# Inverse Fourier transform along the tokens with k and -k in two halves of the partitions, exchanged by DMA and combined before a real-matrix product

## The chip, the core and the metric

The kernel runs on one core of a Trainium2 chip. The metric is the device time of one execution in microseconds (us); the median of three runs of the kernel before is 484.28 us (483.43 to 484.54).

## What is computed

The input x has 2048 tokens of 448 features. It is normalized per token, and three things are added: x itself, a gated network of the normalized input, and a spectral filter of it.

```python
xn = layernorm(x)
X  = rfft2(xn, axes=(tokens, features))      # 2048 x 225 complex
A  = irfft2(X * (w_r + 1j * w_i))            # 2048 x 448 real
gate, up = xn @ W_gate, xn @ W_up            # 448 -> 1792
B  = (gate * (gate > 0) * up) @ W_down       # 1792 -> 448
out = x + A + B
```

The change is in the inverse transform along the tokens, a part of A.

## The kernel before

**The two works.** The gated network is the foreground: 56 units of two wide products each (`gu_unit`, 14 blocks of 128 hidden features times four chunks of 512 tokens), written as fp16 high and low parts so that three fp16 products stand for one fp32 product, and products back to 448 columns (`dn_mm`, 48 of them). After each unit ACT and DVE turn its PSUM tile into `h` (`gu_post`); that tile has two buffers, so unit i+2 waits for the post of unit i. The spectral filter is the background: a list `bg` of steps, each with a cost. `run_bg` hands them out after each foreground unit, in the list's order, so many cost units for each unit; the pace is the sum of all costs divided by the foreground's length. A scheduler then lays each engine's instructions out, and each engine runs its own list strictly in order. All loads and stores are issued by SP, in one list too.

**The spectral filter.** The 2048 tokens are split as 16 n1 + n2. Forward: a transform along the features (`f_dft`), one along n1 by matrices of 128 x 128 (`f_sdft`, six stationary matrices for each n2), and four stages of butterflies over n2 on DVE (`bfly`). Then 16 products with the weights (`wmul`, the weights come by `load_wf`), the four butterfly stages backwards (`inv1`, `stage2`, `stage3`, `stage4`), which give one tile U for each n2, [128 partitions of k1, 4 groups x 2 (real, imaginary) x 57], and then, for each n2, a chain of seven steps, the list `il`:

- `i_hi` (ACT, line 460) and `i_lo` (DVE, lines 466 and 467): U as fp16 high and low part into `vt`, which has two buffers. Line 467 writes a negated copy of the imaginary part beside them, so that `vt` holds (-imaginary, real, imaginary) for each group.
- `i_sdft` (PE, line 479): the complex transform along k1. `vt` is stationary, the constant `im` (cosine and sine, high and low: four 128 x 128 matrices, loaded by `load_im`, line 453, three buffers) moves. For each of four groups three products with the cosine and three with the sine: 24 matmuls for each n2.
- `i_pq`, `i_pqlo` (ACT and DVE, lines 485 to 498), `i_ddft` (PE, line 507, 12 matmuls), `i_acc` (DVE, line 512): the inverse along the features, added onto the output tile `xy`.

In step t of that part each item of `il` runs for another n2, the last item first, and every second step begins with a `stage4` that makes two tiles U.

```python
seq = ((0, cw, 0), (0, cw, 2), (1, cw, 0), (0, sw, 1), (0, sw, 3), (1, sw, 1))
for i, (h, w, c) in enumerate(seq):
    P.matmul(o, v[:, h, w], m[:, c, :], start=(i == 0), stop=(i == 5), skip_group_check=True)
```

The names of the lines in the profile: L590 and L597 `gu`, L638 `dn`, L479 `i_sdft`, L507 `i_ddft`, L332 to L336 `f_sdft`, L623 and L626 the DVE part of `gu_post`, L644 `dn_post`, L343 to L367 the butterflies, L438 to L441 `wmul`.

Of the kernel before, what the change touches and what calls it, by code (L numbers as in the profile page):

```python
# [9 lines left out]
F16 = mybir.dt.float16  # L10
F32 = mybir.dt.float32
# [8 lines left out]
KC = 57  # L20
GW = 2 * KC
XW = 4 * GW
VW = 3 * KC
VT = 700
GROUPS = [5, 5, 4]
BGEND, LAG, AHEAD, RAMP = 10, 1, 3, 5
NWARM = 24
# [34 lines left out]
    return off, GW * 15  # L62


def _constants():
# [46 lines left out]
    ident = np.eye(128, dtype=np.float16)  # L112
    return dict(ident=ident, c_fd=c_fd, c_fm=c_fm, c_im=c_im, c_id=np.ascontiguousarray(c_id))


@with_exitstack
def tile_gfnet_reglu(ctx: ExitStack, tc: tile.TileContext, x, xr, wgu, wd, wf, ident, c_fd, c_fm, c_im, c_id, out):
    nc = tc.nc
    V, A, P, G = nc.vector, nc.scalar, nc.tensor, nc.gpsimd

# [206 lines left out]
    def f_sdft(n2):
        ps = fx()
        y = ps[:, 0:XW].rearrange("p (g c k) -> p g c k", g=4, c=2)
        m, xh = fm_t[n2], Xh[n2]  # L330
        for i, (a, b) in enumerate(((0, 0), (0, 1), (3, 0))):
            P.matmul(y, m[:, a, :], xh[:, b], start=(i == 0), stop=False, skip_group_check=True)  # L332
        for a, b in ((1, 0), (1, 1), (4, 0)):
            P.matmul(y[:, :, 0], m[:, a, :], xh[:, b, :, 1], start=False, stop=True, skip_group_check=True)  # L334
        for a, b in ((2, 0), (2, 1), (5, 0)):
            P.matmul(y[:, :, 1], m[:, a, :], xh[:, b, :, 0], start=False, stop=True, skip_group_check=True)  # L336
        yps[n2] = y

    def bfly(a, b, p, sgn):

# [108 lines left out]
    sps, pg, pgh, vt = {}, {}, {}, {}  # L449

    def load_im(n2):
        im_t[n2] = it([128, 4, 128], F16, "im", 3)
        nc.sync.dma_start(im_t[n2], c_im[n2])

    def i_hi(n2):
        v = vt[n2] = state["vt"][state.setdefault("vn", 0) % 2]
        state["vn"] += 1
        u = cur["U", n2].rearrange("p g c k -> p g (c k)")
        g = v[:, :, 0:4 * VW].rearrange("p h (g w) -> p h g w", g=4)
        A.activation(g[:, 0, :, KC:], u, AF.Copy, scale=fsc[:, 0:1])  # L460

    def i_lo(n2):
        ut = cur.pop(("U", n2))
        u = ut.rearrange("p g c k -> p g (c k)")
        g = vt[n2][:, :, 0:4 * VW].rearrange("p h (g w) -> p h g w", g=4)
        V.scalar_tensor_tensor(g[:, 1, :, KC:], u, fsc[:, 0:1], g[:, 0, :, KC:], op0=OP.mult, op1=OP.subtract)  # L466
        V.tensor_scalar(g[:, :, :, 0:KC], g[:, :, :, 2 * KC:], -1.0, None, op0=OP.mult)
        free.append(ut)

    def i_sdft(n2):  # L470
        ps = fx()
        v, m = vt[n2], im_t[n2]
        for g in range(4):
            o = ps[:, 128 * g:128 * (g + 1)]
            cw = slice(VW * g + KC, VW * g + KC + 128)
            sw = slice(VW * g, VW * g + 128)
            seq = ((0, cw, 0), (0, cw, 2), (1, cw, 0), (0, sw, 1), (0, sw, 3), (1, sw, 1))
            for i, (h, w, c) in enumerate(seq):
                P.matmul(o, v[:, h, w], m[:, c, :], start=(i == 0), stop=(i == 5), skip_group_check=True)  # L479
# [225 lines left out]
    fft_chunk(3)  # L705
    add(0.3, wmax_scale)
    add(0.0, open_inv)
    add(0.0, lambda: nc.sync.dma_start(idc_t, c_id))
    ks = [0, 4, 2, 6, 1, 5, 3, 7]
    korder = [k for k0 in ks for k in (k0, k0 + 8)]  # L710
# [1 line left out]
        add(0.0, load_wf, k)  # L712
    add(0.0, wneg, korder[0])
    nload = 3
    for k0 in ks:
        add((1.1, 1.7, 1.7, 1.7, 1.2, 1.7, 1.7, 1.7)[k0], stage4, k0, 1, "s3", "X")
        for k in (k0, k0 + 8):
            i = korder.index(k)
            if i + 1 < 16:
                add(0.0, wneg, korder[i + 1])  # L720
            add(1.7, wmul, k)
            if nload < 16:
                add(0.0, load_wf, korder[nload])
                nload += 1
        add(1.1, inv1, k0)
        if k0 >= 4:
            for par in range(2):
                add(1.1 + 0.1 * par, stage2, k0 - 4, par, -1, "i1", "i2")
            if k0 - 4 >= 2:
                for k in range(4):  # L730
                    add((1.1, 1.7, 1.2, 1.7)[k], stage3, k0 - 6, k, -1, "i2", "i3")
# [267 lines left out]
```

## Time and profile before

| what | value |
|---|---|
| median of three runs | 484.28 us |
| the profiled execution's own time | 483.15 us |
| its span, first to last instruction | 481.2 us |
| mean granted TensorE clock | 0.991 |
| inverse transforms on PE (L479) | 346.95 to 453 us of the span |
| foreground left behind the last background matmul | 460.4 to 477.5 us |

A profile shows one execution. For each engine it gives the time in which it was busy; the views used below are the page's summary, the stretches (busy time of each engine in a piece of the span), the timeline (instructions in order of time: start, duration, engine, line, operation, tiles, count), the waits (who waited for whom), the chain of waits that ended last, and the DMA issues with their time to landing. A matmul's duration in it includes the way through the array, so what one costs PE in a row of many is the distance from start to start, not that duration. PEld is TensorE's weight load, SPq is SP's list of DMA issues.

### The profile page before, as it was taken

The page shows a single profiled execution, that of the slowest core. Times are in us where ns is not written, and L with a number is a line of the kernel's source. Part 1 is how long each engine was busy: PE and PEld are TensorE (multiplying, and loading weights), DVE is VectorE, ACT ScalarE, POOL GpSimd, SP SyncE. Part 2 cuts the span into 40 slices and gives each one's busy share as a digit, 9 for nine tenths or more (in the row PEclk, how much of TensorE's full clock was granted, in tenths as well). Part 3 has the DMA queues.
Part 4 walks back from the last instruction along what each step waited for, and adds up shares of the span by engine and source line. Part 5 has one row for each costly group of instructions (what it writes and reads, how often), then busy time and mean ns, then how long its engine had stood idle before and what let it go on. Part 6 is the DMA issues. An engine that isn't in the chain of part 4 may idle for free.

```text
span 481.2 us, 7678 instructions
## 1 busy us (share of the span) xinstructions
PE 467.2 (97%) x2896; PEld 245.6 (51%) x2896; DVE 384.3 (80%) x934; ACT 170.3 (35%) x341; POOL 28.9 (6%) x62
## 2 busy tenths in 40 slices
PE   8769999999999999999999999999999999999996
PEld 3424455455545555554444444444556565665653
DVE  6779369568964999989999999999998677676632
ACT  5846225132442742332122043442253243333310
POOL 2104004000300100000000000001000000000000
PEclk9898999999999999999999999999999999999999
DMA  7999300601501355150212011200011100020012
GB/s 262 385 380 230 121 1 17 138 0 34 121 1 44 125 173 166 53 180 21 59 41 58 1 39 40 64 2 0 1 33 32 42 23 11 23 72 30 26 71 97
DMA packets 35293, 38.70 MB, mean 80 GB/s; under 512 B 15302, under 2 KB 31430, under 8 KB 35256
## 3 DMA queue, kind: packets, MB, share of 16 engines
q1 hardware_dynamic: 35256, 38.21, 26.0%
q8 instruction: 23, 0.38, 0.3%
q14 instruction: 14, 0.11, 0.1%
HBM read 31.38 MB, written 3.67 MB: 73 GB/s over the span
## 4 chain that ended last, share of the span: by engine, by line
PE 80%; issue 8%; DMA 3%; DVE 2%; ACT 1%; SPq 1%; POOL 0%; POOLq 0%; ACTq 0%
PE gu L590 42%; PE dn L638 24%; PE fx L479 4%; PE fx L507 3%; PE gu L597 3%; PE fx L290 2%; DMA T<-tt 2%; PE fx L332 1%; DMA wst<-in_wgu 1%; PE fx L334 1%; PE fx L336 1%; ACT wt L549 1%; SPq L264 1%; DVE wdm L555 1%; DVE wt L550 0%
## 5 line engine op out<-in xcount | busy, mean ns | idle before, releaser
L590 PE MATMUL gu<-T,wt 128*128 128x512 f16 (+1 forms) x1140 | 257.0, 378 | 4.6 <-DVE T L278 2.8
L590 PEld LDWEIGHTS <-wt 128*128 128x128 f16 x1140 | 109.9, 98 | 134.8 <-issue 14.9
L638 PE MATMUL dn<-wdt,h 128*128 128x448 f16 x672 | 134.8, 352 | 0.0
L638 PEld LDWEIGHTS <-h 128*128 128x128 f16 x672 | 65.4, 98 | 60.7 <-issue 1.3
L622 ACT ACTIVATE g<-gu 128x512 f32<-128x512 f32 x56 | 33.3, 595 | 119.2 <-PE gu L597 70.3
L623 DVE SCALAR_TENSOR_TENSOR g<-gu,g 128x512 f32<-128x512 f32 x56 | 38.4, 685 | 23.0 <-ACT g L622 22.9
L625 ACT ACTIVATE h<-g 128x512 f16<-128x512 f32 x56 | 35.0, 626 | 37.6 <-DVE g L623 35.3
L644 DVE SCALAR_TENSOR_TENSOR xy<-dn,dsc,xy 128x448 f32<-128x448 f32 x48 | 32.4, 679 | 18.1 <-PE dn L638 18.1
L626 DVE TENSOR_TENSOR h<-g,h 128x512 f16<-128x512 f32 x56 | 38.4, 686 | 9.8 <-ACT h L625 9.6
L466 DVE SCALAR_TENSOR_TENSOR vt<-y,fsc,vt 128x456 f16<-128x456 f32 x16 | 11.0, 690 | 17.8 <-ACT vt L460 17.8
L479 PEld LDWEIGHTS <-vt 128*128 128x128 f16 x384 | 22.7, 98 | 3.5
L479 PE MATMUL fx<-im,vt 128*128 128x128 f16 x384 | 23.9, 219 | 0.0
L549 ACT ACTIVATE wt<-wst,wsc 128x512 f16<-128x512 f32 x28 | 18.9, 712 | 13.3 <-DVE wsc L541 11.8
L550 DVE SCALAR_TENSOR_TENSOR wt<-wst,wsc,wt 128x512 f16<-128x512 f32 x28 | 20.4, 745 | 3.4 <-ACT wt L549 3.4
L597 PE MATMUL gu<-T,wt 64*128 64x512 f16 x112 | 17.0, 381 | 4.2 <-DVE wt L550 4.0
L527 ACT ACTIVATE junk<-wst 128x512 bf16<-128x512 f32 x28 | 17.4, 622 | 6.1 <-DMA wst<-in_wgu 5.8
L495 ACT ACTIVATE pgh<-pg 114x512 f16<-114x512 f32 x16 | 10.1, 628 | 26.4 <-DVE pg L493 26.4
L460 ACT ACTIVATE vt<-y,fsc 128x456 f16<-128x456 f32 x16 | 10.7, 674 | 22.3 <-PE fx L479 22.3
L530 POOL PARTITION_ALL_REDUCE wm<-wm x15 | 7.3, 485 | 160.0 <-ACT junk L527 160.0
L507 PE MATMUL fx<-idc_t,pgh 114*128 114x112 f16 (+1 forms) x192 | 16.6, 236 | 0.0
L322 ACT ACTIVATE Xh<-X 128x456 f16<-128x456 f32 x16 | 9.3, 579 | 18.5 <-DVE X L320 9.5
L344 DVE TENSOR_TENSOR y<-y,y 128x456 f32<-128x456 f32 x22 | 13.9, 630 | 0.5
(102 smaller groups left out, 458.0 us busy)
## 6 DMA issues: line engine op xcount, KB each, us to landing
wst<-in_wgu SPq DMA_DIRECT2D x28, 256.0 KB, 4.2
wmx<-in_wf SPq DMA_DIRECT2D x16, 228.0 KB, 2.7
wf<-in_wf SPq DMA_DIRECT2D x16, 228.0 KB, 2.5
y<-in_xr SPq DMA_DIRECT2D x16, 224.0 KB, 5.0
xy<-in_x SPq DMA_DIRECT2D x16, 224.0 KB, 5.1
out<-xy SPq DMA_DIRECT2D x16, 224.0 KB, 1.9
wdst<-in_wd SPq DMA_DIRECT2D x14, 224.0 KB, 4.1
fm<-in_c_fm SPq DMA_DIRECT2D x16, 192.0 KB, 2.6
```

The lines of the kernel that those rows point to most:

```text
L479: P.matmul(o, v[:, h, w], m[:, c, :], start=(i == 0), stop=(i == 5), skip_group_check=True)
L507: P.matmul(ps[:, o0:o1], h[:, a, i, :], idc_t[:, b, c0:c0 + o1 - o0], start=(j == 0 and i < 3), stop=True, skip_group_check=True)
L549: A.activation(w[:, 0:4, :], st, AF.Copy, scale=sc)
L550: V.scalar_tensor_tensor(w[:, 4:8, :], st, sc, w[:, 0:4, :], op0=OP.mult, op1=OP.subtract)
L590: last["P"] = P.matmul(hps[f, q][:, g, cs], wt[f, g][:, a, :], Tq[q][:, b, cs], start=(start and i == 0), stop=(stop and i == len(seq) - 1 ...
L597: m = P.matmul(hps[f, q][:, g, 0:512], wt[f, g][rows, 7, :], Tq[q][rows, b, :], start=start, stop=not start).ins
L622: last["A"] = A.activation(g1, hps[f, q][:, 0, :], AF.Relu, scale=2.0 ** -22).ins
L623: last["V"] = V.scalar_tensor_tensor(g1, hps[f, q][:, 1, :], 2.0 ** -22, g1, op0=OP.mult, op1=OP.mult).ins
L625: A.activation(h[:, 0, :], g1, AF.Copy)
L626: V.tensor_tensor(h[:, 1, :], g1, h[:, 0, :], op=OP.subtract)
L638: last["P"] = P.matmul(ps[:, 0:D], ht[f, q][:, a, js], wdt[f][:, b, :], start=(i == 0), stop=(i == n - 1)).ins
L644: last["V"] = V.scalar_tensor_tensor(xy[:, n2, :], dps[n2][:, 0:D], dsc[:, g:g + 1], xy[:, n2, :], op0=OP.mult, op1=OP.add).ins
```

## The change

The frequencies are laid out anew over the partitions: partition p holds k1 = p for p up to 64, and k1 = -(p - 64) for p from 65 to 127. So k and -k are 64 partitions apart. The forward matrices of the upper half have sine and cosine in each other's place, so that the forward half runs the same instructions on other constants. In the inverse half:

- `i_swap` (new, SP): for each n2 three DMAs: row 64 of U is replaced by a row of a tile `row` (line 510), partitions 65 to 127 of U go to partitions 1 to 63 of a tile t (line 513), and 1 to 63 to 65 to 127 (line 514). There are three tiles t, in the place of the weight buffers `wf`.
- `i_pair` (new, DVE, lines 518 and 519): two operations of 128 x 228 that subtract and add t.
- `i_lo` loses the negated copy; `vt` holds each group once.
- `i_sdft` has three matmuls for each group, 12 for each n2, with one real matrix (high and low); `load_im` loads half as much.
- Row 64 (k1 = 64, its own partner) takes another way: after each `wmul` a DMA copies it to one of 16 partitions of `row` (`row_in`, line 482); once, `row_hi`, `row_lo` and `row_dft` put it through a 16-point transform (nine matmuls of the forms of `f_sdft`) and `row_ev` writes it back to `row`.
- The background steps stand in another order around this: `inv1` and what follows for one k come a step later, behind the next `wmul`; `load_im` comes two steps later. The costs of the steps are changed, most of them raised (butterflies of 1.7 count 2.0, `wmul` 2.0).

```diff
+    def row_in(k2):
+        if "row" not in state:
+            state["row"] = it([16, 4, 2, KC], F32, "row")
+        nc.sync.dma_start(state["row"][k2:k2 + 1], cur["V", k2][64:65])
...
+    def row_dft():
+        ps = fx()
+        y = state["rowps"] = ps[0:16, 0:XW].rearrange("p (g c k) -> p g c k", g=4, c=2)
+        cdft(y, row_t, state["rowh"])
...
+    def i_swap(n2):
+        u = cur["U", n2]
+        nc.sync.dma_start(u[64:65], state["row"][n2:n2 + 1])
+        t = sw[n2] = state["sw"][state.setdefault("swn", 0) % 3]
+        state["swn"] += 1
+        nc.sync.dma_start(t[1:64], u[65:128])
+        nc.sync.dma_start(t[65:128], u[1:64])
+
+    def i_pair(n2):
+        u, t = cur["U", n2], sw[n2]
+        V.tensor_tensor(u[:, :, 0], u[:, :, 0], t[:, :, 1], op=OP.subtract)
+        V.tensor_tensor(u[:, :, 1], u[:, :, 1], t[:, :, 0], op=OP.add)
...
-        V.tensor_scalar(g[:, :, :, 0:KC], g[:, :, :, 2 * KC:], -1.0, None, op0=OP.mult)
...
-            seq = ((0, cw, 0), (0, cw, 2), (1, cw, 0), (0, sw, 1), (0, sw, 3), (1, sw, 1))
-            for i, (h, w, c) in enumerate(seq):
-                P.matmul(o, v[:, h, w], m[:, c, :], start=(i == 0), stop=(i == 5), skip_group_check=True)
+            w = slice(GW * g, GW * g + 128)
+            for i, (h, c) in enumerate(((0, 0), (0, 1), (1, 0))):
+                P.matmul(o, v[:, h, w], m[:, c, :], start=(i == 0), stop=(i == 2), skip_group_check=True)
...
-    il = ((0.0, i_hi), (0.8, i_lo), (0.0, i_sdft), (1.4, i_pq), (0.6, i_pqlo), (0.0, i_ddft), (0.7, i_acc))
+    il = ((0.0, i_swap), (0.8, i_pair), (0.0, i_hi), (0.7, i_lo), (0.0, i_sdft), (1.4, i_pq), (0.7, i_pqlo),
+          (0.0, i_ddft), (0.7, i_acc))
```

Two places of the order show what moves. The first is DVE's list at the first inverse transforms of the kernel before, from the last `stage4` butterfly (L343, L344, which write two tiles U, here `y_81` and `y_71`) to the end of `i_lo` for the first of them.

```order
L343 TENSOR_TENSOR y_81<-y_74,y_71 128x456
L344 TENSOR_TENSOR y_71<-y_74,y_71 128x456
L623 SCALAR_TENSOR_TENSOR g_3731<-gu,g_3731 128x512
L466 SCALAR_TENSOR_TENSOR vt_2538<-y_81,fsc,vt_2538 128x4x114
L466 SCALAR_TENSOR_TENSOR vt_2539<-y_71,fsc,vt_2539 128x4x114
L467 TENSOR_SCALAR vt_2538<-vt_2538 128x2x4x57
```

In the changed kernel the same place reads as follows; `y_68` is the first tile U, L685 and L688 are `gu_post`, L706 is `dn_post`, L380 and L381 belong to the next butterfly, `wf` is the tile t.

```order
L363 TENSOR_TENSOR y_68<-y_74,y_71 128x456
L706 SCALAR_TENSOR_TENSOR xy<-dn,dsc,xy 128x448
L364 TENSOR_TENSOR y_71<-y_74,y_71 128x456
L688 TENSOR_TENSOR h<-g_3554,h 128x512
L706 SCALAR_TENSOR_TENSOR xy<-dn,dsc,xy 128x448
L380 SCALAR_TENSOR_TENSOR y_74<-y_81 128x4x57
L381 SCALAR_TENSOR_TENSOR y_74<-y_81 128x4x57
L518 TENSOR_TENSOR y_68<-y_68,wf 128x4x57
L519 TENSOR_TENSOR y_68<-y_68,wf 128x4x57
L386 SCALAR_TENSOR_TENSOR y_81<-y_74,y_75 128x456
L387 SCALAR_TENSOR_TENSOR y_75<-y_74,y_75 128x456
L531 SCALAR_TENSOR_TENSOR vt_2442<-y_68,fsc,vt_2442 128x456
```

Between the write of U and the fp16 low part there stand now six other rows, then the pair (L518, L519), then two rows of the next butterfly. The second place is SP's list where the inverse transforms begin. Before, it holds loads of weights and of `im` only:

```order
L175 DMA wst<-in_wgu 128x512 x2
L453 DMA im<-in_c_im 128x512 x4
L648 DMA out<-xy 128x448
L453 DMA im<-in_c_im 128x512
L648 DMA out<-xy 128x448
```

In the changed kernel (L510, L513, L514 the three DMAs of a swap, L473 `load_im`):

```order
L195 DMA wst<-in_wgu 128x512 x2
L482 DMA row<-y_71 1x12x38
L510 DMA y_68<-row 1x12x38
L513 DMA wf<-y_68 63x456
L514 DMA wf<-y_68 63x456
L510 DMA y_71<-row 1x12x38
L513 DMA wf<-y_71 63x456
L514 DMA wf<-y_71 63x456
```

Where two loads and no transfer inside the core stood, three transfers for each n2 stand now: five swaps follow one another so, and behind them `load_im` and the stores of `out` stand among the swaps.

More of the change, by code (lines that the diff above doesn't have):

```diff
@@ L22 @@
 XW = 4 * GW
-VW = 3 * KC
-VT = 700
+VT = XW + 14
 GROUPS = [5, 5, 4]
@@ L62, in _fd_parts, with _freqs @@
     return off, GW * 15
+def _freqs():
+    p = np.arange(128)
+    k1 = np.where(p < 64, p, np.where(p == 64, 64, 64 - p))
+    return (k1[None, :] + 128 * np.arange(16)[:, None]) % S
 def _constants():
@@ L325, in f_lo, with cdft @@
         V.tensor_tensor(Xh[n2][:, 1], X[n2], Xh[n2][:, 0], op=OP.subtract)
[L327 to L330, printed above, removed]
+    def cdft(y, m, xh):
         for i, (a, b) in enumerate(((0, 0), (0, 1), (3, 0))):
@@ L336, in f_sdft @@
             P.matmul(y[:, :, 1], m[:, a, :], xh[:, b, :, 0], start=False, stop=True, skip_group_check=True)
-        yps[n2] = y
+    def f_sdft(n2):
+        y = yps[n2] = fx()[:, 0:XW].rearrange("p (g c k) -> p g c k", g=4, c=2)
+        cdft(y, fm_t[n2], Xh[n2])
     def bfly(a, b, p, sgn):
@@ L451, in load_im, with row_hi, row_lo, row_ev @@
     def load_im(n2):
-        im_t[n2] = it([128, 4, 128], F16, "im", 3)
+        im_t[n2] = it([128, 2, 128], F16, "im", 3)
         nc.sync.dma_start(im_t[n2], c_im[n2])
+    def row_in(k2):
+        if "row" not in state:
+            state["row"] = it([16, 4, 2, KC], F32, "row")
+        nc.sync.dma_start(state["row"][k2:k2 + 1], cur["V", k2][64:65])
+    def row_hi():
+        h = state["rowh"] = it([16, 2, 4, 2, KC], F16, "rowh")
+        A.activation(h[:, 0], state["row"], AF.Copy, scale=fsc[0:16, 0:1])
+    def row_lo():
+        h = state["rowh"]
+        V.scalar_tensor_tensor(h[:, 1], state["row"], fsc[0:16, 0:1], h[:, 0], op0=OP.mult, op1=OP.subtract)
+    def row_dft():
+        ps = fx()
+        y = state["rowps"] = ps[0:16, 0:XW].rearrange("p (g c k) -> p g c k", g=4, c=2)
+        cdft(y, row_t, state["rowh"])
+    def row_ev():
+        V.tensor_scalar(state["row"], state["rowps"], small[0:16, 19:20], 2.0 ** -10, op0=OP.mult, op1=OP.mult)
+    def open_swap():
+        state["sw"] = [it([128, 4, 2, KC], F32, "wf", 3) for _ in range(3)]
+        for t in state["sw"]:
+            for p in (0, 64):
+                G.memset(t[p:p + 1], 0.0)
+    sw = {}
+    def i_swap(n2):
[9 more added lines that the diff above has]
+        V.tensor_tensor(u[:, :, 1], u[:, :, 1], t[:, :, 0], op=OP.add)
     def i_hi(n2):
@@ L457, in i_hi @@
         state["vn"] += 1
-        u = cur["U", n2].rearrange("p g c k -> p g (c k)")
-        g = v[:, :, 0:4 * VW].rearrange("p h (g w) -> p h g w", g=4)
-        A.activation(g[:, 0, :, KC:], u, AF.Copy, scale=fsc[:, 0:1])
+        u = cur["U", n2].rearrange("p g c k -> p (g c k)")
+        A.activation(v[:, 0, 0:XW], u, AF.Copy, scale=fsc[:, 0:1])
     def i_lo(n2):
         ut = cur.pop(("U", n2))
[L464 to L467, printed above, removed]
+        u = ut.rearrange("p g c k -> p (g c k)")
+        v = vt[n2]
+        V.scalar_tensor_tensor(v[:, 1, 0:XW], u, fsc[:, 0:1], v[:, 0, 0:XW], op0=OP.mult, op1=OP.subtract)
         free.append(ut)
@@ L714, in tile_gfnet_reglu, with back @@
     nload = 3
-    for k0 in ks:
-        add((1.1, 1.7, 1.7, 1.7, 1.2, 1.7, 1.7, 1.7)[k0], stage4, k0, 1, "s3", "X")
+    def back(k0):
+        add(1.2, inv1, k0)
+        if k0 >= 4:
+            for par in range(2):
+                add(1.25 + 0.3 * par, stage2, k0 - 4, par, -1, "i1", "i2")
+            if k0 - 4 >= 2:
+                for k in range(4):
+                    add((1.25, 2.0, 1.55, 2.0)[k], stage3, k0 - 6, k, -1, "i2", "i3")
+    for i0, k0 in enumerate(ks):
+        add((1.25, 2.0, 2.0, 2.0, 1.55, 2.0, 2.0, 2.0)[k0], stage4, k0, 1, "s3", "X")
         for k in (k0, k0 + 8):
@@ L720, in tile_gfnet_reglu @@
                 add(0.0, wneg, korder[i + 1])
-            add(1.7, wmul, k)
+            add(2.0, wmul, k)
+            add(0.0, row_in, k)
             if nload < 16:
@@ L724, in tile_gfnet_reglu @@
                 nload += 1
[L725 to L731, printed above, removed]
-    il = ((0.0, i_hi), (0.8, i_lo), (0.0, i_sdft), (1.4, i_pq), (0.6, i_pqlo), (0.0, i_ddft), (0.7, i_acc))
+        if i0:
+            back(ks[i0 - 1])
+    add(0.0, open_swap)
+    add(0.0, row_hi)
+    add(0.6, row_lo)
+    back(ks[-1])
+    add(0.0, row_dft)
+    add(0.6, row_ev)
+    il = ((0.0, i_swap), (0.8, i_pair), (0.0, i_hi), (0.7, i_lo), (0.0, i_sdft), (1.4, i_pq), (0.7, i_pqlo),
+          (0.0, i_ddft), (0.7, i_acc))
     io = [n for n0 in range(8) for n in (n0, n0 + 8)]
@@ L735, in tile_gfnet_reglu @@
         if t < 16 and t % 2 == 0:
-            add(1.7, stage4, t // 2, -1, "i3", "U")
-        if t < 16:
-            add(0.0, load_im, io[t])
+            add(2.0, stage4, t // 2, -1, "i3", "U")
+        if 2 <= t < 18:
+            add(0.0, load_im, io[t - 2])
         for st in reversed(range(len(il))):
```

35 lines of the change are left out of this document (23 added, 12 removed).

## The prediction

> **What bounds the kernel now.** I read the page's busy times first, then its chain of waits, then the stretches.
>
> ```profile
> PE 467.2 (97%) x2896; PEld 245.6 (51%) x2896; DVE 384.3 (80%) x934; ACT 170.3 (35%) x341; POOL 28.9 (6%) x62
> ...
> PE 80%; issue 8%; DMA 3%; DVE 2%; ACT 1%; SPq 1%; POOL 0%; POOLq 0%; ACTq 0%
> ```
>
> PE is busy in 97% of the span and makes 80% of the chain that ended last; DVE makes 2%. The stretches say where the missing 3% are (length, then busy time of PE, PEld, DVE, ACT, POOL, each with its count; granted clock, DMA share, GB/s).
>
> ```profile
> 0.00:40.00 40.00, 30.30 (x160) 15.57 (x161) 30.50 (x101) 24.80 (x53) 7.64 (x29) 0.91 0.96 334
> ...
> 240.00:280.00 40.00, 40.00 (x197) 18.07 (x196) 38.56 (x79) 9.07 (x19) 0.00 (x0) 1.00 0.11 30
> 280.00:320.00 40.00, 40.00 (x199) 18.22 (x198) 39.35 (x92) 17.96 (x41) 2.23 (x4) 1.00 0.15 43
> 320.00:345.00 25.00, 25.00 (x125) 11.36 (x124) 24.69 (x53) 6.51 (x11) 1.83 (x1) 1.00 0.00 1
> 345.00:370.00 25.00, 25.00 (x209) 15.22 (x207) 22.59 (x57) 11.67 (x22) 0.00 (x0) 1.00 0.08 23
> 370.00:400.00 30.00, 30.00 (x249) 18.23 (x248) 20.55 (x49) 9.55 (x18) 0.00 (x0) 1.00 0.10 34
> ```
>
> PE idles 9.7 us in the first 40 us, which the change does not touch; in the rows from 240 to 400 us it idles not at all, at full clock. DVE nearly fills 240 to 345 us (102.6 of 105 us) and then has slack: 2.4 us in 345 to 370, 9.5 us in the next 30. So what PE no longer has to do in the inverse part shortens the kernel, as long as DVE, which gets more to do just behind its fullest stretch, does not make PE wait there.
>
> **What goes.** The timeline of PE around one inverse transform (start, duration, what, count):
>
> ```profile
> 357.35 1.50 PE L479 MATMUL fx<-im,vt 128*128 128x128 f16 x24
> 358.69 1.03 PE L507 MATMUL fx<-idc_t,pgh 114*128 114x112 f16 x12
> ...
> 360.19 4.27 PE L590 MATMUL gu<-T,wt 128*128 128x512 f16 x19
> 364.30 1.50 PE L479 MATMUL fx<-im,vt 128*128 128x128 f16 x24
> ```
>
> From start to start 24 matmuls take 1.34 us, 55.8 ns each (the 1.50 us hold the way through the array behind the last one). The change takes 12 of 24 in each of 16 transforms: 192 x 55.8 ns = **10.7 us** of PE. PE is the bound there, so all of it counts. The Trainium skill ("TensorE: Matmul & The Clock Gate", section "Back-to-back issue gap") gives about 81 ns as the sustained distance of such 128-column matmuls with their weight loads; by it 15.6 us would go and the result, all else as below, would be near 471 us on the scale of the median. This trace has 55.8 ns, weight loads included, and the trace decides.
>
> On DVE the negated copy goes: 16 operations, each 0.19 us from start to start (first two rows below), 3.0 us. Half the loads of `im` go too; they were early anyway and are worth nothing.
>
> **What comes on PE.** `row_dft` has nine matmuls of the three forms of one `f_sdft`, three of each; it has fewer partitions, but what streams is as wide.
>
> ```profile
> 112.69 0.74 PE L332 MATMUL fx<-Xh,fm 128*128 128x456 f16 x3
> 113.27 0.47 PE L334 MATMUL fx<-Xh,fm 128*128 128x228 f16 x3
> 113.58 0.46 PE L336 MATMUL fx<-Xh,fm 128*128 128x228 f16 x3
> 113.88 0.92 PE L638 MATMUL dn<-wdt,h 128*128 128x448 f16 x4
> ```
>
> From the first row's start to the last row's that is **1.19 us**, once. PE's balance is 10.7 - 1.2 = 9.5 us less.
>
> **What comes on DVE, and what hides it.**
>
> ```profile
> 342.82 0.28 DVE L467 TENSOR_SCALAR vt<-vt 128x456 f16<-128x456 f16 x1
> 343.01 0.39 DVE L360 SCALAR_TENSOR_TENSOR y<-y 128x228 f32<-128x228 f32 x1
> 343.31 0.39 DVE L361 SCALAR_TENSOR_TENSOR y<-y 128x228 f32<-128x228 f32 x1
> ```
>
> `i_pair` has two fp32 operations of 128 x 228; such an operation takes 0.39 us, 0.30 from start to start. 32 of them are 9.6 us, and `row_lo` and `row_ev` are as long as a 456-wide operation, 0.55 each (L344 to L623 below): 10.7 us come, 3.0 go, 7.7 us more, 0.5 us in each step of the inverse part. A step takes some 7 us (357.35 to 364.30 above), so 370 to 400 us hold about four, and DVE idles 9.45 us there, 2.4 us a step; each step also gets 0.67 us shorter. About 1.2 us a step of cover are left, so in the steady part I count the pairs at nothing. Were that cover gone, their 9.6 us would be PE's.
>
> **The swap's wait.** No plain copy from SBUF to SBUF has a row here. The loads of `im` land 2.0 us after their issue, those of `wf` 2.5, the transposing transfers within SBUF 3.3, and the slowest `fm` 5.2 (minimum, median, maximum in the fourth row; the fifth is that of `im`); the last row gives SP's spacing, (2.16 - 0.33)/3 = 0.61 us from one issue to the next.
>
> ```profile
> im<-in_c_im SPq DMA_DIRECT2D x16, 128.0 KB, 2.0
> wf<-in_wf SPq DMA_DIRECT2D x16, 228.0 KB, 2.5
> ...
> T<-tt SPq DMA_TRANSPOSE x12, 3.3
> ...
> DMA to landing us min/median/max: 2.2/2.6/5.2
> DMA to landing us min/median/max: 1.9/2.0/3.2
> ...
> 21.03 2.16 SPq L169 DMA_DIRECT2D y<-in_xr  x4
> ```
>
> A swap's third DMA is issued 1.2 us after the first and lands 2.0 to 2.5 us later: 3.2 to 3.7 us after U is written. I take 3.5, since a half moves 115 KB and transposes nothing, nearest to `im`; bounds 3.1 (1.9, `im`'s shortest and no row's less) and, with 5.2, 6.4; as slow as a transpose it would be 4.5. L518 stands in DVE's list and waits for it, with the posts L685 and L688 queued behind it and PE's next units waiting for those. In the order quoted above, the first L518 has seven rows between U's write and itself, the write counted: two `dn_post` and one `gu_post` operation of 0.60, two butterflies of 0.55, two of 0.30, in all 3.5 us. So the first swap is just covered at 3.5, short by 1.0 us at 4.5 and by 2.9 us at 6.4. On SP the swap queues `load_im` and `out` behind it: `im` has three buffers and was ready long before, and eleven stores stand behind the last swap in any case. `row_in` stands before `load_wf` on SP and waits for `wmul`, whose next weights are three tiles ahead: nothing.
>
> **The first transforms** are the tight place. Before:
>
> ```profile
> 339.79 0.63 DVE L343 TENSOR_TENSOR y<-y,y 128x456 f32<-128x456 f32 x1
> 340.46 0.64 DVE L344 TENSOR_TENSOR y<-y,y 128x456 f32<-128x456 f32 x1
> 340.63 1.23 ACT L460 ACTIVATE vt<-y,fsc 128x456 f16<-128x456 f32 x2
> 341.01 0.68 DVE L623 SCALAR_TENSOR_TENSOR g<-gu,g 128x512 f32<-128x512 f32 x1
> 341.61 1.29 DVE L466 SCALAR_TENSOR_TENSOR vt<-y,fsc,vt 128x456 f16<-128x456 f32 x2
> ...
> 346.95 2.84 PE L479 MATMUL fx<-im,vt 128*128 128x128 f16 x48
> ```
>
> U is written from 339.79, the negated copy ends at 342.82 + 0.28 = 343.10, PE comes at 346.95: 3.85 us of cushion. In the changed kernel the chain from U's write is 3.5 us to the pair, 0.7 for the pair, 0.6 for ACT's high part and 0.7 for the low part (both as before), 5.5 us instead of 3.3: 2.2 us of the cushion go. `row_lo` and `row_ev` take 1.1 more. Left are 0.5 us. How much later DVE gets there because the raised costs hand the background out faster, into a stretch that is 98% full, no row shows. I take **1.0 us** of waiting, near the 0.5 us of cushion; bounds 0 (the cushion holds; waiting cannot gain) and 6 us: a landing of 5.2 us is 2.9 us short at the first swap, and again at the fourth, which needs the first one's tile t.
>
> **The sum**, against the profiled execution's own 483.15 us: -10.7 + 1.2 + 1.0 = -8.5 us, 474.6 us. The median stands 1.13 us above that execution, and so I forecast **475.7 us** for the median.
>
> **The rivals.**
>
> *DVE makes the first stretch longer.* For it: 24.69 of 25 us busy in 320 to 345 us, three swap tiles, U tiles that come two at a time. Against it: the cushion of 3.85 us. Decided by a landing near a transpose's 3.3 us with a DVE that arrives 2 us later: 4 to 5 us lost instead of 1, 478 to 479 on the own scale, about 479.5 for the median. Chance 0.19.
>
> *The exchange becomes the bound: slower.* Each of the 16 pairs waits for its swap. Between U's write and its pair stand 5 to 27 rows of DVE in the changed order, 4.7 us on average by the durations above; DVE's spare 1.2 us a step lie on top. To eat 9.5 us, each step has to lose 0.6 us, so the swap must take 6.5 us, a landing of 5.3 us every time; at a landing of 6.5 us it would be 16 x (1.2 + 6.5 - 5.9) = 29 us against 9.5 gained, near 504 us. For it: only `fm`'s slowest row. Against it: the DMA share there is 0.08 to 0.10, against 0.96 where loads took longest. Chance 0.06.
>
> *PE is not the bound.* Its 97% would be a share of overlapping durations, and the 9.5 us would turn into idle time: 483 to 484 us, no change. The trace speaks against it: 19 `gu` matmuls take 4.11 us from 360.19 to 364.30, 216 ns each, without a gap, and 216 + 55.8 and the like fill every stretch. Chance 0.04. In the Trainium skill, "Perfetto Trace Analysis", section "Identifying the Most-Contended Engine", matmul busy time is called no good measure and the share of weight loads a better one. By that rule PE has half its time to spare (51%) and DVE with 80% binds; the start-to-start distances of this trace do not bear it out.
>
> *More goes than I count*, by closer packing of what is left: 470 to 473 us, chance 0.03.
>
> **How the numbers follow.** The forecast's case has 0.68. Its own range is 474.7 (no wait) to 476.7. The range for 8 in 10 reaches up to the 6 us bound, 483.15 - 9.5 + 6 + 1.1 = 480.7, and down to 473.6, no wait and no offset between profile and median. A measurement tells 0.2% (1 us) from no change: faster 0.68 + 0.19 + 0.03 = 0.90, same 0.04, slower 0.06.
>
> **What would show it.** L479's successor, L541, has 192 matmuls, 12 in 0.67 us from start to start; PE busy falls to about 458 us; the waits of PE name at most a few us for DVE or ACT near 345 to 360 us; the swaps land in 2.0 to 2.5 us; DVE's busy time rises to about 392 us, and its waits for them sum to a few us. Wrong would be: PE idle between 370 and 440 us, waits of DVE for the swaps above 1 us each, or a PE that is as full and no earlier done.

## The result, and the profile after

| | before | after |
|---|---|---|
| median, beside each other on one chip | 484.11 us (13 runs, 483.42 to 484.97) | 480.81 us (13 runs, 478.76 to 483.58) |
| the profiled execution: own time, span | 483.15, 481.2 us | 480.81, 479.0 us |
| mean granted clock | 0.991 | 0.989 |

The ratio is 0.9928, with a 95% interval of 0.9911 to 0.9945. The kernel got 3.3 us faster, where 8.5 were forecast; 480.81 lies just outside the range (473.6 to 480.7). The runs of after spread over 1%, those of before over 0.3%.

The page's busy times after, and the start of its chain:

```profile
PE 460.4 (96%) x2713; PEld 235.9 (49%) x2713; DVE 391.5 (82%) x952; ACT 171.0 (36%) x342; POOL 29.3 (6%) x68
...
PE 51%; DVE 29%; DMA 8%; issue 3%; ACT 2%; POOL 1%; SPq 1%; DVEq 0%; ACTq 0%; POOLq 0%
```

PE lost 6.8 us of busy time and DVE gained 7.2. But the chain that ended last went through PE for 80% of the span and now does for 51%; DVE has 29% instead of 2%. Somewhere PE now waits for DVE. The stretches show where:

```profile
320.00:340.00 20.00, 20.00 (x100) 8.99 (x99) 19.86 (x45) 5.41 (x9) 2.49 (x1) 1.00 0.00 1
340.00:360.00 20.00, 16.39 (x105) 7.96 (x104) 16.88 (x47) 5.71 (x11) 0.00 (x0) 0.99 0.26 80
360.00:380.00 20.00, 20.00 (x133) 10.95 (x132) 18.90 (x45) 9.66 (x18) 0.00 (x0) 0.92 0.20 63
380.00:400.00 20.00, 20.00 (x149) 11.51 (x147) 16.09 (x38) 6.60 (x12) 0.00 (x0) 1.00 0.15 46
```

In 340 to 360 us, at the first inverse transforms, PE idles 3.6 us, and at the same time DVE, which has the most to do just there, idles 3.1 us. From 360 us on PE is full, in the first 20 us at a clock of 0.92. PE's timeline has these gaps behind the ramp (start, duration, what, and in brackets the idle time ahead and who ended it):

```profile
176.76 4.48 PE L652 MATMUL gu<-T,wt 128*128 128x512 f16 x20 [0.81 <-DVE g L685]
181.85 0.61 PE L659 MATMUL gu<-T,wt 64*128 64x512 f16 x4 [0.36 <-DVE g L685]
347.32 0.28 PE L541 MATMUL fx<-im,vt 128*128 128x128 f16 x2 [0.59 <-ACT vt L525]
348.50 0.73 PE L541 MATMUL fx<-im,vt 128*128 128x128 f16 x10 [0.32 <-DVE vt L531]
358.78 5.52 PE L652 MATMUL gu<-T,wt 128*128 128x512 f16 x17 [2.57 <-DVE g L685]
```

The largest, 2.57 us, is no wait for a transform: a foreground unit waits for the post (L685) of the unit two ahead of it. ACT's half of that post began at 353.92; DVE came to it at 358.04. The reason stands in the lists of SP and DVE (L363 writes the first tile U):

```profile
353.92 0.59 ACT L684 ACTIVATE g<-gu 128x512 f32<-128x512 f32 x1
```

```profile
338.87 0.72 SPq L510 DMA_DIRECT2D y<-row  x1
339.65 0.73 SPq L513 DMA_DIRECT2D wf<-y  x1
340.43 0.70 SPq L514 DMA_DIRECT2D wf<-y  x1
341.25 0.74 SPq L510 DMA_DIRECT2D y<-row  x1
```

```profile
338.22 0.62 DVE L363 TENSOR_TENSOR y<-y,y 128x456 f32<-128x456 f32 x1
...
343.43 0.40 DVE L518 TENSOR_TENSOR y<-y,wf 128x228 f32<-128x228 f32 x1 [1.64 <-DMA wf<-y]
...
349.04 0.40 DVE L518 TENSOR_TENSOR y<-y,wf 128x228 f32<-128x228 f32 x1 [0.60 <-DMA wf<-y]
...
351.48 0.40 DVE L518 TENSOR_TENSOR y<-y,wf 128x228 f32<-128x228 f32 x1 [0.46 <-DMA wf<-y]
...
353.94 0.40 DVE L518 TENSOR_TENSOR y<-y,wf 128x228 f32<-128x228 f32 x1 [0.35 <-DMA wf<-y]
...
358.04 0.68 DVE L685 SCALAR_TENSOR_TENSOR g<-gu,g 128x512 f32<-128x512 f32 x1
```

The three transfers of a swap are issued 0.78 us apart, and the pair starts 3.0 us after the third (340.43 to 343.43): 4.56 us from the first issue. Ahead of the post, DVE waits 1.64 + 0.60 + 0.46 + 0.35 = 3.05 us for swaps, the first, third, fourth and fifth. From the first write of U to the post its list takes 19.82 us, 16.7 without the waits. In the whole run DVE waits 11.7 us for swaps, at ten of the sixteen pairs; the other 8.6 us lie behind 375 us, where PE is full, and cost PE nothing. Then the clock (stretches of one microsecond):

```profile
357.00:358.00 1.00, 0.00 (x0) 0.00 (x0) 1.00 (x3) 0.00 (x0) 0.00 (x0) 1.00 0.00 0
...
360.00:361.00 1.00, 1.00 (x4) 0.41 (x3) 1.00 (x5) 0.71 (x2) 0.00 (x0) 0.50 0.49 144
361.00:362.00 1.00, 1.00 (x4) 0.30 (x2) 1.00 (x2) 0.63 (x1) 0.00 (x0) 0.50 0.32 98
362.00:363.00 1.00, 1.00 (x4) 0.37 (x3) 1.00 (x5) 0.62 (x2) 0.00 (x0) 0.50 0.13 38
363.00:364.00 1.00, 1.00 (x6) 0.47 (x5) 1.00 (x3) 1.00 (x3) 0.00 (x0) 0.92 0.46 150
```

Behind the gap half the clock is granted for more than 3 us: the 17 matmuls take 5.35 us (358.78 to 364.13), 315 ns each instead of 216, 1.7 us more. In sum PE idles 4.65 us behind the ramp (the first 60 us), where before it idled 0.35, and loses 1.7 us to the clock. A gap costs PE a little more than its idle time: a `gu` matmul lasts 0.38 us in the profile and the next can start 0.216 us after it, so 0.16 us more go with each gap.

### The profile page after: what moved, and what is told of

It is laid out like the page before. It is cut to its first block, busy times and chain, and to the rows that moved or that the text cites. A ratio compares the mean times of both kernels' runs of the same rounds, so it can differ in the third digit from the quotient of the medians.

```text
span 479.0 us, 7506 instructions
## 1 busy us (share of the span) xinstructions
PE 460.4 (96%) x2713; PEld 235.9 (49%) x2713; DVE 391.5 (82%) x952; ACT 171.0 (36%) x342; POOL 29.3 (6%) x68
## 4 chain that ended last, share of the span: by engine, by line
PE 51%; DVE 29%; DMA 8%; issue 3%; ACT 2%; POOL 1%; SPq 1%; DVEq 0%; ACTq 0%; POOLq 0%
PE gu L652 23%; PE dn L700 16%; PE fx L569 3%; DVE g L685 3%; PE fx L310 3%; DMA wmx<-in_wf 2%; DVE h L688 2%; DVE wt L612 2%; DVE xy L706 2%; DMA wf<-in_wf 2%; DVE y L363 2%; PE fx L541 2%; DVE y L364 2%; DMA wf<-y 2%; DVE y L458 2%
## 5 line engine op out<-in xcount | busy, mean ns | idle before, releaser
L685 DVE SCALAR_TENSOR_TENSOR g<-gu,g 128x512 f32<-128x512 f32 x56 | 38.3, 683 | 17.8 <-ACT g L684 17.8
L688 DVE TENSOR_TENSOR h<-g,h 128x512 f16<-128x512 f32 x56 | 38.2, 685 | 7.3 <-ACT h L687 7.1
L706 DVE SCALAR_TENSOR_TENSOR xy<-dn,dsc,xy 128x448 f32<-128x448 f32 x48 | 32.5, 678 | 10.9 <-PE dn L700 10.8
L452 ACT ACTIVATE wf<-wf 128x114 f32<-128x114 f32 x16 | 4.8, 298 | 35.8 <-DMA wf<-in_wf 26.8
L518 DVE TENSOR_TENSOR y<-y,wf 128x228 f32<-128x228 f32 x16 | 6.3, 393 | 11.7 <-DMA wf<-y 11.7
L541 PEld LDWEIGHTS <-vt 128*128 128x128 f16 x192 | 11.9, 98 | 5.7 <-DVE vt L531 1.3
L541 PE MATMUL fx<-im,vt 128*128 128x128 f16 x192 | 13.7, 219 | 1.0 <-ACT vt L525 0.6
## 6 DMA issues: line engine op xcount, KB each, us to landing
wf<-y SPq DMA_DIRECT2D x32, 112.2 KB
```

The costliest lines, as they stand in the source:

```text
L685: last["V"] = V.scalar_tensor_tensor(g1, hps[f, q][:, 1, :], 2.0 ** -22, g1, op0=OP.mult, op1=OP.mult).ins
L688: V.tensor_tensor(h[:, 1, :], g1, h[:, 0, :], op=OP.subtract)
L706: last["V"] = V.scalar_tensor_tensor(xy[:, n2, :], dps[n2][:, 0:D], dsc[:, g:g + 1], xy[:, n2, :], op0=OP.mult, op1=OP.add).ins
```

## The experiments

Three theories at the start. **W**: the waits for the swaps in DVE's list make the post late. **D**: DVE's added work makes it late. **C**: the raised costs of the background steps, and the order that follows, do. Each time below is a median, with the ratio to the kernel before in the same session and its 95% interval. The changed kernel has 0.9911 to 0.9945: `e1_dummy` lies above that, `e2_act`, `e3_rows64`, `e11_nopair` and the last three below it, and the other seven overlap with it.

**The transfers taken out of the pair's way** (`e1_dummy`): the same three transfers, but between tiles that nobody reads; the pair adds zeros, so the exchange itself is left out.

```diff
-        nc.sync.dma_start(u[64:65], state["row"][n2:n2 + 1])
+        nc.sync.dma_start(d[64:65], state["row"][n2:n2 + 1])
-        nc.sync.dma_start(t[1:64], u[65:128])
-        nc.sync.dma_start(t[65:128], u[1:64])
+        nc.sync.dma_start(t[1:64], d[65:128])
+        nc.sync.dma_start(t[65:128], d[1:64])
-        u, t = cur["U", n2], sw[n2]
+        u, t = cur["U", n2], state["zero"]
```

> The exchange is cut: the same 48 transfers per execution run between tiles that nobody waits for, and each pair adds a tile of zeros, so DVE does the same work (the output leaves the partner frequencies out). Theory W (the swaps' wait in DVE's list makes the post of one unit late, PE stalls 2.6 us there and runs at half clock behind it): the 11.7 us of DVE waiting on the swaps go, PE has no gap above 0.5 us between 340 and 365 us and full clock there, and the time is 475 to 477 us. Rival D (DVE's added work alone overfills the stretch): PE still stalls 2 us or more near 355 us, and the time stays at 479 to 481. Rival C (the raised costs, which make PE wait near 176 us, cost most of it): the stalls near 176 us stay, and the time stays at 479 to 481.

483.17 us, 0.9979 (0.9966 to 0.9992): slower than after. The trace says why this test is a bad one. Transfers that wait for nothing no longer stay in place on SP:

```profile
322.15 0.70 SPq L519 DMA_DIRECT2D wf<-dummy  x1
322.89 0.73 SPq L482 DMA_DIRECT2D row<-y  x1
323.73 0.73 SPq L518 DMA_DIRECT2D wf<-dummy  x1
```

They start at 299.93 us and from 316 us on fill SP's list without a pause, 0.7 us each, and the last copies for the row's transform stand between them. That transform comes late, and PE waits 2.18 + 0.36 us for it and 2.53 us for the post behind. From 340 to 460 us, at the first transforms, PE has no gap. This fits W and does not prove it.

**The row's transfer left out** (`e4_norow`), so that row 64 keeps its own values, **and with it 64 rows a half instead of 63** (`e3_rows64`), where rows 0 and 64 are exchanged as well. These two have the same instructions on every engine (a few neighbours stand in another order); only the rows of the transfers differ.

```diff
-        nc.sync.dma_start(u[64:65], state["row"][n2:n2 + 1])
...
-        nc.sync.dma_start(t[1:64], u[65:128])
-        nc.sync.dma_start(t[65:128], u[1:64])
+        nc.sync.dma_start(t[0:64], u[64:128])
+        nc.sync.dma_start(t[64:128], u[0:64])
```

> The first of the three transfers of a swap (the row of k1 = 64) is left out, so row 64 goes on untransformed; a swap costs SP two issues of 0.78 us instead of three. Theory W: the chain from U to its pair is 3.8 us instead of 4.6, DVE waits on the swaps 4 to 7 us in all instead of 11.7, the stall of PE near 356 us shrinks by a half or more, 477 to 479 us. Rival D: no change, 480 to 481. Rival C: no change, 480 to 481.

> As the kernel without the row transfer, but each half moves 64 rows instead of 63 (rows 0 and 64 get partners they should not have). Every list of instructions is the same otherwise. If the 3.0 us from issue to use come from how 63 rows are spread over the transfer engines, the issue gets shorter than 0.7 us or the landing falls to 2.0 to 2.5 us, DVE's waiting on the swaps falls by a half or more against the run without the row transfer, and the time falls by 0.5 to 1.5 us. If a transfer within SBUF is as slow anyway, nothing changes between the two.

479.27 us, 0.9901 (0.9880 to 0.9921), and 476.70 us, 0.9838 (0.9822 to 0.9854). The kernel without the row has this gap, and the lists of SP and DVE of the kernel with 64 rows read as follows:

```profile
357.21 3.02 PE L651 MATMUL gu<-T,wt 128*128 128x512 f16 x8 [2.71 <-DVE g L684]
```

```profile
339.33 0.54 SPq L512 DMA_DIRECT2D wf<-y  x1
339.96 0.54 SPq L513 DMA_DIRECT2D wf<-y  x1
340.61 0.54 SPq L512 DMA_DIRECT2D wf<-y  x1
```

```profile
338.64 0.62 DVE L363 TENSOR_TENSOR y<-y,y 128x456 f32<-128x456 f32 x1
...
342.27 0.40 DVE L517 TENSOR_TENSOR y<-y,wf 128x228 f32<-128x228 f32 x1
...
355.38 0.69 DVE L684 SCALAR_TENSOR_TENSOR g<-gu,g 128x512 f32<-128x512 f32 x1
```

With 63 rows the issues take 0.70 to 0.75 us and the chain of two is 3.8 us (338.44 to 342.25 in `e4_norow`); with 64 rows an issue takes 0.46 to 0.59 us and the median landing is 2.2 us. From the second issue to a pair that waits for it, it is 3.0 us (339.24 to 342.25) against 2.3 (379.47 to 381.80). With 64 rows DVE hardly waits for a swap ahead of the post (0.06 us in all; later 2.6 us at three pairs, where PE is full), and the gap in front of the unit goes from 2.71 to 1.39 us:

```profile
356.12 3.61 PE L651 MATMUL gu<-T,wt 128*128 128x512 f16 x16 [1.39 <-DVE g L684]
```

Behind 1.39 us the clock stays at 1.0. With the same instructions 2.6 us hang on the transfers alone. And the waits add up: from the first write of U to the post DVE's list takes 18.68 us in `e4_norow` with 1.80 us of waiting, and 16.74 with 64 rows; less the waits, that is 16.8 and 16.7 us, as in the changed kernel (16.7). So the post comes late by what DVE waits, which is W. That the gap of `e4_norow` is 2.71 us all the same, and not half of 2.57 as expected, lies with PE: it waits less at the transforms and comes to the unit at 354.50 us instead of 356.21. The 1.39 us that are left without waits are not W's.

What makes the transfer of 64 rows shorter is not settled: its halves also begin at rows 0 and 64 instead of 1 and 65, and no run separates the two. The Trainium skill, "DMA: Bandwidth & Descriptors", section "Why a DMA increments its semaphore by 16 and not by 1", says that a transfer is split over the largest number of engines up to 16 that divides its rows; by that rule it would be 9 for 63 rows and 16 for 64. The two durations agree with it; which engines carried them no view shows.

**The third transfer issued by ACT** (`e2_act`).

```diff
-        nc.sync.dma_start(t[65:128], u[1:64])
+        nc.scalar.dma_start(t[65:128], u[1:64])
```

> The third transfer of each swap is issued by ACT instead of SP, side by side with the other two; the result is whole. Theory W: a swap occupies SP for 1.6 us instead of 2.35, the chain is 3.8 us or less instead of 4.6, DVE waits 4 to 7 us in all on the swaps, 477 to 479 us, if ACT (36% busy) hides its 0.7 us issues. Rivals D and C: no change, 480 to 481, or slower by what ACT's posts lose.

478.84 us, 0.9880 (0.9863 to 0.9897). The gap of 2.57 us is gone, but a DMA issue that waits for U holds ACT's own list (two issues in each row):

```profile
341.40 2.34 ACTq L514 DMA_DIRECT2D wf<-y  x2
...
349.67 3.31 ACTq L514 DMA_DIRECT2D wf<-y  x2
```

PE waits 0.59 and 1.01 us at the first transforms, where the changed kernel waits 0.59 and 0.32.

**The row off the chain, with the whole result** (`e6_early`): the row goes into row 64 of t, as soon as t is free, and the pair takes it from there. **And a pause in the list ahead of the first pairs** (`e7_pause`), **and the second half on GpSimd** (`e8_pool`).

```diff
+        nc.sync.dma_start(t[64:65], state["row"][n2:n2 + 1])
...
-        V.tensor_tensor(u[:, :, 0], u[:, :, 0], t[:, :, 1], op=OP.subtract)
+        V.scalar_tensor_tensor(u[:, :, 0], u[:, :, 0], m, t[:, :, 1], op0=OP.mult, op1=OP.subtract)
```

```diff
+        if t == 1:
+            add(3.0, lambda: None)
```

```diff
-        nc.sync.dma_start(t[65:128], u[1:64])
+        nc.gpsimd.dma_start(t[65:128], u[1:64])
```

> The whole computation. The row of k1 = 64 no longer goes into U behind its write: it goes into row 64 of t as soon as t is free, and the pair multiplies U by a column that is 1, at partition 64 it is 0, so that the row comes in with the subtraction and addition that are there anyway. One transfer of three (0.78 us of SP) leaves the chain from U to the pair; the length of DVE's list is the same but for one more operation of 16 partitions. Theory W (the swaps' wait in DVE's list makes a unit's post late): as the kernel without the row, 479.3, between 478.5 and 480.3, with waits of DVE for wf<-y of 8 to 9 us in sum. Theory D (DVE's added work alone): as the changed kernel, 480.8. Theory C (raised costs and the order): 480.8.

> As e6_early, and a pause of 3.0 cost units is put into the background list between the first swaps and the first pairs, so that the foreground's posts and the pairs stand in another order in DVE's list there. No transfer and no operation changes. Theory W: the wait at the first swaps goes below 0.3 us each and with it the gap of 2.6 us before a foreground unit near 357 us and the half clock behind it, some 4 us in all: 475 to 477. Theory D: DVE has the same work, no gain against e6_early, 479 to 481. Theory C: a part of the gain of W, since the background is handed out slower at this place, 477 to 479.

> As e6_early, with the second half of each swap issued by GpSimd, which is 6% busy, beside the first half on SP. Theory W: the chain from U to the pair is 0.75 us shorter than in e6_early if GpSimd's issue costs no more than SP's: 477 to 478.5; if GpSimd's transfers land a microsecond later than SP's: 479 to 481. Theories D and C: no change from e6_early.

481.44 us, 0.9948 (0.9929 to 0.9968); 479.62, 0.9911 (0.9892 to 0.9930); 479.49, 0.9905 (0.9883 to 0.9927). The chain got shorter as expected, 3.8 us, and 3.1 with GpSimd, but `e6_early` gained nothing. Its lists show two new costs:

```profile
348.30 2.21 SPq L516 DMA_DIRECT2D wf<-row  x2
```

```profile
344.98 0.46 DVE L523 SCALAR_TENSOR_TENSOR y<-y,keep,wf 128x228 f32<-128x228 f32 x1
```

A row's transfer that waits until t is free holds SP, for 2.21 us with two issues here, and with it the next swaps; and the operation with a column of factors takes 0.46 us instead of 0.39. The unit's gap is 3.99 us. With the pause that gap goes, but a stall of 1.45 us at the transform along the features comes (and 1.28 us near 177 us): 1.8 us less than `e6_early`, and not the 475 to 477 that W gave. In `e8_pool` the pairs wait 0.19 and 0.53 us only, and the gap is still 2.96 us: twelve operations longer by 0.07 us, 0.8 us in all, stand ahead of the post, and PE comes to the unit 1.6 us earlier (354.58 us). So in this stretch DVE's work counts as its waits do.

**The costs of before** (`e5_costs`): butterflies, `wmul` and `inv1` as they were.

```diff
-            add(2.0, wmul, k)
+            add(1.7, wmul, k)
...
-            add(2.0, stage4, t // 2, -1, "i3", "U")
+            add(1.7, stage4, t // 2, -1, "i3", "U")
```

> The changed kernel with the costs of the background steps that the change raised (butterflies, wmul, inv1) set back to their values of before; nothing else. Theory C (the raised costs hand the background out faster into stretches where DVE is full): the stall of 1.2 us near 176 us goes, and the first inverse transforms get a foreground post between U and the pair: 477 to 479. Theory W: DVE's waits for the swaps stay at 1.6, 0.6, 0.5 and 0.4 us at the first four, 480 to 481. Theory D: 480.8.

481.28 us, 0.9947 (0.9928 to 0.9966). C falls, as far as these costs go (the order of the steps was not put back): the stall near 176 us goes, as C said, but the one post that now stands between U and the pair brings nothing, since PE waits elsewhere (0.77 us at 194, 1.44 at 355, 0.87 at 376, 1.10 at 425, 0.96 at 453 us). That less was handed out ahead and more is late would explain it; it was not traced.

**The pairs on GpSimd** (`e9_gpair`), and **no pairs at all** (`e11_nopair`, which transforms U unpaired).

```diff
-        V.tensor_tensor(u[:, :, 0], u[:, :, 0], t[:, :, 1], op=OP.subtract)
-        V.tensor_tensor(u[:, :, 1], u[:, :, 1], t[:, :, 0], op=OP.add)
+        G.tensor_tensor(u[:, :, 0], u[:, :, 0], t[:, :, 1], op=OP.subtract)
+        G.tensor_tensor(u[:, :, 1], u[:, :, 1], t[:, :, 0], op=OP.add)
```

> The changed kernel with the two operations of each pair on GpSimd instead of DVE; nothing else, the whole computation. DVE loses 32 x 0.30 = 9.6 us of work and has no wait for the transfers in its list; GpSimd, 6% busy, waits for them. Theory W+D (waits and pairs together lengthen DVE's list between two foreground posts near 341 to 358 us by 3.0 + 3.5 us): the gap of 2.6 us there and the half clock behind it go, 475 to 477. If an operation of 128 x 228 takes GpSimd 2 us or more, PE's first transforms wait some 3 us longer each: 478 to 482. If neither waits nor pairs are the cause (raised costs, order): 480 to 481.

> The changed kernel without the pairs' two operations; the transfers are still issued, nothing waits for them but the reuse of their tiles, and the transforms take U unpaired. Theory W+D: as e9_gpair without GpSimd's part, no gap near 357 us, 474 to 476.5, which is what the forecast gave without its waiting (474.7) and less. Theory C (raised costs and order): 479 to 481. Theory W without D and D without W can't be told apart here.

481.01 us, 0.9934 (0.9914 to 0.9953), and 476.74 us, 0.9848 (0.9829 to 0.9868). GpSimd is no slow one (0.74 and 0.76 us on the mean), but the wait did not leave DVE's list; it moved to the next row that needs the pair:

```profile
346.55 0.69 DVE L531 SCALAR_TENSOR_TENSOR vt<-y,fsc,vt 128x456 f16<-128x456 f32 x1 [2.33 <-ACT vt L525]
```

The kernel without pairs is as fast as the one with 64 rows, in which the pairs are done and the waits are gone (476.74 and 476.70). So D, as the cause by itself, falls: with all of the pairs' work in DVE's list some 4 us go. But the equality is one of totals. PE's gaps are others: `e11_nopair` has none at the unit, but 0.67 and 0.44 us at the first transforms and 1.16 us near 177, where the kernel with 64 rows has 1.39 us at the unit and 0.37 near 177. So the pairs' work seems to have a share in that 1.39 us.

**PE's gap filled** (`e10_warm`): eight matmuls that nothing reads.

```diff
+            if gpos[i] == 44:
+                wps = psum.tile([128, 512], F32, name="dn", bufs=2)
+                keep = [P.matmul(wps, warm[:, 0:128], warm, start=True, stop=True) for _ in range(8)]
```

> The changed kernel with eight matmuls of 128 x 512 on a constant tile, into a spare bank, put into PE's list right where it waits 2.57 us for the late post near 356 us; they are extra work that nothing reads. DVE's list up to there is the same. Theory H (behind that gap the granted clock is 0.50 to 0.72 for some 3.4 us, and this costs 1.7 us): the eight fill 1.7 us of the gap, the clock stays at 1.0 and the next 17 matmuls take 3.7 us instead of 5.4: 479.1, between 478.3 and 479.8. If the clock is not set by the gap, 480.8; if the eight come on top of the gap, 482.5.

481.42 us, 0.9943 (0.9927 to 0.9959): no gain. PE's timeline:

```profile
356.93 1.89 PE L1008 MATMUL dn<-warm 128*128 128x512 f16 x8
359.89 2.10 PE L652 MATMUL gu<-T,wt 128*128 128x512 f16 x9 [1.08 <-DVE g L685]
```

The clock stayed at 1.0, the nine matmuls took 216 ns each, and yet 1.36 us of waiting for DVE (L574) came back at 378 us. So the half clock is a consequence of the gap. That its 1.7 us can't be had back by themselves, since DVE is behind and a faster PE waits for it later, is what this run suggests and does not prove: in its profiled execution one swap's wait was 1.72 us instead of 0.46, ahead of the eight matmuls, and the post stood at 359.15 us instead of 358.04.

**The chain shorter, the pace changed, and both.** `f2_pool` issues the row and the second half on GpSimd, `f1_pace` counts the costs of the first eight inverse steps double, `f3_both` does both; all with the whole result.

```diff
-        nc.sync.dma_start(u[64:65], state["row"][n2:n2 + 1])
+        nc.gpsimd.dma_start(u[64:65], state["row"][n2:n2 + 1])
...
-        nc.sync.dma_start(t[65:128], u[1:64])
+        nc.gpsimd.dma_start(t[65:128], u[1:64])
```

```diff
-            add(2.0, stage4, t // 2, -1, "i3", "U")
+            add(2.0 * (2.0 if t < 8 else 1.0), stage4, t // 2, -1, "i3", "U")
...
-                add(il[st][0], il[st][1], io[i])
+                add(il[st][0] * (2.0 if t < 8 else 1.0), il[st][1], io[i])
```

> The changed kernel with two of the three transfers of a swap (the row and the second half) issued by GpSimd beside the first half on SP; operations and costs are the same. From U's write to the pair it should be 3.1 us as in e8_pool instead of 4.6. Theory W: the waits at the first swaps go below 0.3 us each, the post that PE waits for comes some 2.5 us earlier, the gap of 2.57 us goes below 1 us: 477 to 478.5. Theory D: the gap stays, 480 to 481.

> The changed kernel with the costs of the inverse steps counted double for the first eight of them, so that the background is handed out at half the pace around the first swaps and faster later; a foreground post now stands between the second and the third pair in DVE's list. Operations and transfers are the same. Theory W+D (DVE is late in 341 to 358 us by its pairs and by its waits for the swaps, and has room later): 477 to 479. Theory W alone (only the waits count, whatever stands in the list): the first waits stay, 479.5 to 481. If the place doesn't matter, 480.8.

> f1_pace and f2_pool together. Theory W+D: 475.5 to 477.5, and no gap of PE above 1 us behind 340 us. Theory W alone: as f2_pool, 477 to 478.5. If neither counts, 480.8.

477.92 us, 0.9874 (0.9857 to 0.9891); 477.18, 0.9858 (0.9844 to 0.9871); **475.33, 0.9819 (0.9805 to 0.9832)**. GpSimd's list in `f2_pool`:

```profile
339.55 0.69 POOL L510 DMA_DIRECT2D y<-row  x1 [6.92 <-DVE y L363]
340.24 0.55 POOL L514 DMA_DIRECT2D wf<-y  x1
340.77 0.52 POOL L510 DMA_DIRECT2D y<-row  x1
```

GpSimd's issues run beside SP's, and the first four pairs wait for nothing; the gap is 1.25 us, about what the kernel with 64 rows has, and not below 1 us as expected. In `f1_pace` the first pairs still wait, 0.80 + 1.49 + 0.46 us, but a post stands between them (341.02 us), and PE's only gap there is 1.10 us at a transform. As the pace follows from the sum of the costs, this edit also hands out all that stands ahead faster: the first pair comes at 337.01 us instead of 343.43. So a wait in DVE's list costs what the posts behind it can't spare, and both ways of help work: shorten it, or leave room. In `f3_both`:

```profile
340.00:360.00 20.00, 20.00 (x140) 10.70 (x137) 20.00 (x57) 9.65 (x18) 5.21 (x10) 1.00 0.23 69
360.00:380.00 20.00, 20.00 (x145) 11.84 (x142) 18.72 (x43) 6.76 (x13) 3.12 (x6) 1.00 0.22 69
```

PE and DVE are both full through the first transforms; behind the ramp PE has one gap left, 0.59 us near the end. It is faster than before by 1.8%, and its interval lies clear of after's.

## Why the prediction was wrong

- **What goes, right.** L541's 12 matmuls take 0.67 us from start to start (378.00 to 378.67). Where next to nothing waits, PE's balance of 9.5 us comes out nearly whole: `f3_both`, with one gap of 0.59 us left, is 8.9 us below before by the medians of its session (484.27 and 475.33), 8.1 by the two profiled spans.
- **The row's transfer, right.** 1.19 us were counted; from 323.38 to 324.66 us it is 1.28.
- **The pairs in the steady part cost nothing, right.** PE is full from 365 to 460 us. DVE has 3.9 us of slack in 380 to 400, and 2.9 of these are waits for swaps.
- **The swap's wait: mis-sized.** 3.5 us were taken from U to the pair; it is 4.56. SP's spacing came from loads (0.61 us; these transfers: 0.78, twice) and the landing from `im` (2.0; here 3.0). The bounds, 3.1 to 6.4, held it, and the working even said "short by 1.0 us at 4.5" (measured 1.64). The 0.6 us between these two are the write of U, which was counted among the rows that cover the swap: the swap starts behind it (338.22 to 338.87).
- **The first transforms: the step that failed.** The 1.0 us of waiting was weighed against the cushion of the transforms, and there it came out, 0.59 + 0.32 us; in part by luck, as the swap took 1.1 us longer than was taken for it. But the same waits stand ahead of a foreground post in DVE's list, and the posts were named and not priced. One swap's shortfall was counted, where four of the first five fall short, 3.05 us, since SP needs 2.35 us for each swap (347.06 to 349.41). PE lost 2.57 us at the unit and 1.7 us to the clock, which had no term in the sum: 5.2 us in this stretch instead of 1.0.
- **A stall that was not in the sum.** 0.81 + 0.36 us near 176 to 182 us, where before had no gap; nothing was counted there, and no reason given. It moves with the costs (`e5_costs` has none there, but one at 194 us); `f3_both` has none. Which step of the order makes it was not tried.
- **How the difference adds up.** With this stall, the row's 0.1 us and the 0.35 us of waiting that went, 5.1 of the 6.2 us between 474.6 and 480.81 are named (4.2 + 1.17 + 0.1 - 0.35). The rest is near what a gap costs beyond its idle time: 0.16 us at each of the five, the same back for the one of before, and two short ones, 0.06 and 0.07 us, ahead of the first transforms (344.89 and 346.00 us), in all 1.1 us, an estimate from the distances of the matmuls.
- **The signs.** Of what the prediction named as signs, PE's busy time (460.4) and DVE's (391.5) came near and PE did not idle between 370 and 440 us; but the swaps landed in 3.0 us and not 2.0 to 2.5, DVE's waits for them sum to 11.7 us and not a few, and five of them are above 1 us, a sign of being wrong.
- **The rivals.** "DVE makes the first stretch longer" came in its size, with 5.2 us instead of 4 to 5, and with the forward stall on top that took the time out of the range. Of its two conditions one held, a landing near 3.3 us (3.0); DVE did not come 2 us later: it wrote the first U at 338.22 us instead of 339.79, and against PE, which came to the first transform at 344.89 us instead of 346.95, it was 0.5 us later. That PE is not the bound, by the busy share of the weight loads, was not borne out: PE's matmuls set the time in `f3_both`.

## What to carry to other kernels

A wait put into a list that runs in order is to be priced at everything queued behind it, not only at the consumer it feeds: here the transform had its cushion, and the post of another work, further down the list, had none. The same kind of wait, 8.6 us of it, cost nothing later, where DVE had slack. An engine that is busy in 19.86 of the 20 us ahead has no way to make up for even 3 us; shorten the wait, or thin out the list around it, and do both where each gives half. And an experiment that takes a dependence away also frees the instruction to move: look at the order of the queue before its time is read.

## What had not been expected of the hardware

- 63 rows against 64 in a transfer of nearly the same bytes (112.2 and 114.0 KB): 0.70 to 0.75 us of issue against 0.46 to 0.59, about 3.0 us until the pair can start against 2.3. The first row differs too (1 or 65 against 0 or 64).
- A gap of PE of 2.57 us was followed by half the clock over 3 us; so were 2.71, 2.96 and 3.99 us (`e4_norow`, `e8_pool`, `e6_early`: 0.50 for 3 us each), while 1.39 us was not. The Trainium skill, "TensorE: Matmul & The Clock Gate", section "What's actually happening", has the slow state follow on an idle window of about 3.4 us; three of these gaps are shorter.
- A DMA issued by GpSimd took 0.51 to 0.69 us of its list, and its half had landed within 2.5 us of its issue (340.24 to 342.77 in `f2_pool`, where the pair did not wait), against SP's 3.0.
